# Batch 0 of an attention kernel with two feed-forward layers: v in sixteen transfers, dilated heads by halves of the sequence, and two leading feature tiles on 288, then 224 columns

## The chip, the cores and the metric

The kernel runs on one core of a Trainium2 chip. The metric is the device time of one execution in microseconds (us), as the median of several runs; lower is better. A profile belongs to one execution and gives the start and length of every instruction and of every DMA packet on that core. Five engines work side by side and wait for each other through semaphores only: PE (TensorE, matmuls; its weight loads are listed as PEld), DVE (VectorE), ACT (ScalarE), POOL (GpSimd) and SP (SyncE, here only a queue that issues DMAs). Each engine takes its instructions strictly in the order of its own list.

## The reference

Attention over 4 batches, 8 heads, 576 positions and 64 elements a head, then two feed-forward layers on all 2,304 tokens (512 to 2,048 to 512 elements), all in float32:

```python
scores = q @ k.T / 8                      # per batch and head
mask_plain = (rel >= 0) & (rel < 32)      # heads 0 to 3
mask_dil   = (rel >= 0) & (rel < 128) & (rel % 4 == 0)   # heads 4 to 7
attn = softmax(where(mask, scores, -1e9));  x = attn @ v  # tokens x 512
h = x @ w_in;   x = (h * sigmoid(1.702 * h)) @ w_out      # layer 1
h = x @ w_in2;  out = (relu(h) ** 2) @ w_out2             # layer 2
```

A query of a plain head sees the 32 positions up to its own. A query of a dilated head sees every fourth position of the last 128; the host therefore stores q, k and v of these heads as four runs of 144 positions (positions 0, 4, 8, ..., then 1, 5, 9, ..., and so on), and inside a run the mask is again a band of 32.

## The kernel before, in words

**Layout.** The host lays q and k out transposed and v by windows, for two halves u of 288 positions of each pair of heads (`qkv_in`). The tokens of the feed-forward layers are ordered by the same four runs: the first block of columns (`BLOCKS1[0]`, 512 tokens) holds runs 0, 1 and 2 of batch 0 whole (144 each) and 80 tokens of run 3. So columns 0 to 287 are runs 0 and 1, which for the dilated heads are the first half u = 0 of their stored sequence, and for the plain heads every fourth position from all of the sequence.

**Attention.** `attend` does one sub-step: four row groups of 32 queries (two halves or places of the sequence for two pairs of heads) by `nw` windows of 32 queries. Its chain is `scores` (PE, line 580), `maxima` (DVE, line 598, with the mask of `mask_band`), `exps` (ACT, line 605), the normalisation (lines 643 to 653), `turn` (a DVE transpose, line 667), `values` (PE, line 690, which needs v), and the copies of the result into the x tile as a rounded high part (line 316 or 318) and a remainder (line 707). Batch 0 has four sub-steps, `SUBS0`: windows 0 to 3 and 4 to 8 of both halves of the plain heads, then windows 0 to 4 and 5 to 8 of both halves of the dilated heads. Each pass of `values` waits for the one before it in this order and for the copies that empty its PSUM banks.

**Feed-forward.** `step` is one feature tile f (128 of 2,048 features): 12 `hidden` matmuls (lines 744 to 746; two weight parts and two x parts, four row blocks k of x), `tanh`, `times_h` (line 776), the split into high and remainder (lines 316 and 327), and 12 `project` matmuls (lines 801 to 803), each on up to 512 columns. Row blocks k = 0 and 1 of x are the plain heads, k = 2 and 3 the dilated ones. Weights come as raw tiles (`load_weights`, line 382), whose rounded parts are made by `top`, `join`, `high_part` and `low_part` on ACT and DVE.

**Loads of batch 0.** q and k of the plain heads come in pieces (lines 861 to 864), those of the dilated heads in one transfer for each half (line 884), v in eight transfers of 192 KB (`load_v0`, line 869), six issued by SP and two by ACT. All values of the plain heads wait for four of the eight, all of the dilated heads for the other four; scores of the dilated heads wait for both transfers of line 884.

**The order of all engines** is made in Python while the kernel is built: `Schedule.run` keeps, for each engine, the tasks whose predecessors are done, and takes the one that by its own cost table can start first and, among those about equal, the one with the smallest `want`. Constants such as `T_START`, `OFF`, `LEAD`, `AHEAD` set these wants and so the order alone. It also models eight DMAs in flight (`lanes`), counted over both issuing queues. Where PE would by this plan be idle ahead of the first feature tile, `keep_warm` (line 927) puts matmuls on zeros into its list, one for each 0.18 us (0.36 us in the first 6 us). `HALVES` = 0 means that every feature tile of the first block runs on all 512 columns; `opening` lets tiles 0 and 1 share a pair of PSUM banks so that their k = 0 and 1 matmuls can run before the dilated heads are done.

Of the kernel before, what the change touches and what calls it, by code (L numbers as in the profile page):

```python
# [9 lines left out]
BF16 = mybir.dt.bfloat16  # L10
# [9 lines left out]
P = 128  # L20
# [6 lines left out]
WIN = 32  # L27
KW = 2 * WIN
QB = 96
NBLK = 3  # L30
# [7 lines left out]
UQ, UK, UV = HALF, HALF + PAD, NBLK * P  # L38

T_START = 22.8  # L40
T_ATT = 1.86
# [6 lines left out]
AHEAD = (46, 54, 56)  # L48
# [7 lines left out]
PREP = 11.41  # L56

HALVES = 0
FIRST = 384
RAW_FROM = 2.32  # L60
NEXT_FROM = 22.83
OFF = (0.0, -2.48, 0.0, 0.0, 0.0, 0.0, 4.45, 0.0, 0.0, 0.0, 0.0, -7.43, -2.53, -7.14, -15.14, 0.23, -19.26, 0.0, 6.66, -23.27, 1.18, -0.52, -0.81, -0.26)
SHIFTED = ()
EARLY = 4
V_ACT = (1, 3)
V_PACKET = 0.09
WARM = 256
QK_FROM = -39.99
QK_STEP = 4.17
V_FROM = -22.79  # L70
V_STEP = 7.15
LEAD = (14.75, 2, 2)
# [4 lines left out]
SPARE_POOL = (0, 0, 3.41)  # L77
SPARE_ACT = (0.36, 0.36, 0)
SPARE_TO = (51.64, 211.81)
# [12 lines left out]
    (0, ((0, 0), (1, 0)), 4), (0, ((0, 4), (1, 4)), 5), (1, ((0, 0), (1, 0)), 5), (1, ((0, 5), (1, 5)), 4),  # L92
# [18 lines left out]
X_FROM = 4.93  # L111
X_WANT = 6.41
# [146 lines left out]
def attention_mlp_mlp(  # L259
# [8 lines left out]
    nc = tc.nc  # L268
# [18 lines left out]
    mask_band = att.tile([P, 5, KW], BF16, name="mask_band")  # L287
# [10 lines left out]
    v_first = [staged(f, 4 * NBLK * P).rearrange("k (t d) -> k t d", t=4 * NBLK) for f in (6, 5)]  # L298
# [60 lines left out]
    split_task = {}  # L359
# [42 lines left out]
    def weights(f, part, want, off):  # L402


        m = {}
# [33 lines left out]
        t = task("dma", 1.45, want - LEAD[0] + off[0], load, (), [raw_b], since=RAW_FROM)  # L439
# [18 lines left out]
    def x_pieces(b, pp, u, w0, nw):  # L458
# [3 lines left out]
        q0, q1 = (HALF * u + WIN * w0) // per, (HALF * u + WIN * (w0 + nw)) // per  # L462
        jobs = []
        for n, blk in enumerate(BLOCKS1):
            width = sum(e - a for _, _, a, e in blk)
            runs, col = [], 0
            for bb, r, a, e in blk:
                if bb == b:
                    lo, hi = (a, e) if plain else (r * ROW + a, r * ROW + e)
                    c = col - lo  # L470
                    lo, hi = max(lo, q0), min(hi, q1)
                    if lo < hi:
                        runs.append((r, lo - q0, hi - q0, c + lo))
                col += e - a
# [31 lines left out]
    def mask_of(pp, spec, i):  # L506
        w = spec[0][1] + i
        n = int(w == 0) if pp == 0 else {0: 2, 4: 3, 5: 4}.get(w, 0)
        return mask_band[:, n], n
# [4 lines left out]
    def attend(b, pp, spec, nw, want, n0, loads=None):  # L514
# [51 lines left out]
        def v_of(a, i):  # L566
            if first:
                t = spec[0][1] + i
                v, at = v_first[pp], 4 * NBLK - 1 if t == 3 * NBLK else t % 3 * NBLK + t // 3
            else:  # L570
                v, at = m["v"], i % 3 * 2 + i // 3
            return v[WIN * a:WIN * (a + 1), at]
# [98 lines left out]
        pieces = [(h, piece) for h in (1, 0) for piece in x_pieces(b, pp, *spec[h], nw)]  # L671
# [47 lines left out]
    def step(blk, f, want, a=0, z=None):  # L719
# [74 lines left out]
        for d in range(KD):  # L794

            def project(d=d):
# [10 lines left out]
                split_task[f, 1] + [hi, lo] + blk.setdefault(("last", a, d), []), [gh_b, gl_b, w_b, blk["o_buf"][d]],  # L807
# [34 lines left out]
    def spread_masks(part):  # L842
        n = slice(0, 2) if part == 0 else slice(3, 5)
        for a in (1, 2, 3):
            G.tensor_copy(mask_band[WIN * a:WIN * (a + 1), n], mask_band[0:WIN, n])
        if part == 0:
            G.tensor_copy(mask_band[:, 2], mask_band[:, 1])
            G.tensor_copy(mask_band[P // 2:P, 1], mask_band[P // 2:P, 0])
# [5 lines left out]
    band_tasks.append(band_tasks[0] + [task("pool", 1.1, -1999, lambda: spread_masks(1), mask_loads + band_tasks[0])])  # L854
# [34 lines left out]
    v0 = [[], []]  # L889
    for pp in range(2):  # L890
        for u, k in [(u, k) for u in range(2) for k in range(2)]:
            if pp == 0 and 2 * u + k in V_ACT:
                v0[pp].append(
                    task(
                        "act", 0.45, -900 + 2 * u + k, lambda u=u, k=k: load_v0(0, u, k, A), mask_loads + halves[0][1:], first_bs,
                        move=128 * V_PACKET / 16,
                    )
                )
            else:
                v0[pp].append(  # L900
                    early(
                        128 * V_PACKET / 16, V_FROM + V_STEP * pp + OFF[(8, 10)[u] + pp],
                        lambda u=u, k=k, pp=pp: load_v0(pp, u, k, nc.sync),
                    )
                )
# [648 lines left out]
```

## Time and profile before

| | |
|---|---|
| median of 3 runs | 811.39 us (810.5 to 811.91) |
| the profiled execution | 811.18 us, of which 809.4 us are the span from its first to its last instruction |
| mean granted TensorE clock | 0.994 of full speed |
| busy over the span | PE 98%, PEld 89%, DVE 66%, ACT 50%, POOL 1% |
| first feature matmul (line 744) | starts at 31.94 us |
| DMA | 172.63 MB, 213 GB/s over the span |

The page gives busy time by engine. The timeline lists instructions of one engine in order of time, like ones merged (x says how many), with the idle time before them and what ended it in brackets; "issue" there means that the profile shows nothing that the engine waited for. A queue named SPq or ACTq holds the instructions that issue DMAs. The windows view gives the busy time of each engine in a stretch, and what the DMAs moved.

### The profile page before, as it was taken

How to read it: one execution, taken by the hardware profiler on the slowest of the kernel's cores; microseconds unless marked ns; L12 is line 12 of the kernel's file. 1: busy time of each engine (PE TensorE's matmuls, PEld its weight loads, DVE VectorE, ACT ScalarE, POOL GpSimd, SP SyncE). 2: the span in 40 equal slices, each digit the busy share in tenths (PEclk: the TensorE clock that was granted, in tenths of full speed). 3: DMA queues.
4: the chain of work that ended last, by engine and by line, in shares of the span. 5: the costliest groups of instructions: out<-in, count | busy, mean ns of one | idle time of the engine just before them, and what ended most of it. 6: DMA issues, size and time to landing. Idle time of an engine off the chain costs nothing.

```text
span 809.4 us, 16460 instructions
## 1 busy us (share of the span) xinstructions
PE 796.7 (98%) x6570; PEld 722.4 (89%) x6570; DVE 534.5 (66%) x1170; ACT 406.6 (50%) x931; POOL 5.8 (1%) x17
## 2 busy tenths in 40 slices
PE   6899999999999999999999999999999999999998
PEld 5688888888899988888888999999999999999998
DVE  4788875443355588878887655689455699364774
ACT  5677765344444554444444255446355455354432
POOL 2000000000000000000000000000000000000000
PEclk9799999999999999999999999999999999999999
DMA  9577754221233369989576933695967686677741
GB/s 267 174 236 217 235 164 154 60 54 40 53 112 76 107 221 295 323 289 333 195 271 242 342 119 126 260 354 210 337 242 292 260 314 246 236 270 283 277 187 58
DMA packets 67963, 172.63 MB, mean 213 GB/s; under 512 B 5680, under 2 KB 43568, under 8 KB 62512
## 3 DMA queue, kind: packets, MB, share of 16 engines
q1 hardware_dynamic: 66880, 170.86, 61.3%
q8 instruction: 51, 0.84, 0.4%
q10 hardware_dynamic: 1008, 0.74, 0.3%
q14 instruction: 24, 0.20, 0.1%
HBM read 132.78 MB, written 38.80 MB: 212 GB/s over the span
## 4 chain that ended last, share of the span: by engine, by line
PE 97%; DMA 2%; issue 1%; DVE 0%; ACTq 0%
PE ps L744 8%; PE ps L801 8%; PE ps L745 8%; PE ps L802 8%; PE ps L803 8%; PE ps L746 8%; PE ps L1397 7%; PE ps L1242 7%; PE ps L1398 7%; PE ps L1241 7%; PE ps L1243 7%; PE ps L1396 7%; PE ps L690 2%; DMA first<-in_qkv 2%; PE ps L580 1%
## 5 line engine op out<-in xcount | busy, mean ns | idle before, releaser
L744 PE MATMUL ps<-x,wp 128*128 128x512 f32 (+1 forms) x320 | 119.3, 373 | 0.0
L801 PE MATMUL ps<-gh,wp 128*128 128x512 f32 (+1 forms) x320 | 119.1, 372 | 0.0
L745 PE MATMUL ps<-x,wp 128*128 128x512 f32 (+1 forms) x320 | 117.8, 368 | 0.0
L802 PE MATMUL ps<-gh,wp 128*128 128x512 f32 (+1 forms) x320 | 117.8, 368 | 0.0
L803 PE MATMUL ps<-gl,wp 128*128 128x512 f32 (+1 forms) x320 | 117.7, 368 | 0.0
L746 PE MATMUL ps<-x,wp 128*128 128x512 f32 (+1 forms) x320 | 117.7, 368 | 0.0
L1398 PE MATMUL ps<-gl,ws 128*128 128x384 f32 x336 | 112.2, 334 | 0.0
L1396 PE MATMUL ps<-gh,ws 128*128 128x384 f32 x336 | 112.2, 334 | 0.0
L1397 PE MATMUL ps<-gh,ws 128*128 128x384 f32 x336 | 112.2, 334 | 0.0
L316 ACT CAST gh<-gq 128x768 fp32r<-128x768 f32 x84 | 68.7, 838 | 73.5 <-PE ps L1397 49.8
L327 DVE TENSOR_TENSOR gl<-gq,gh 128x768 fp32r<-128x768 f32 x84 | 80.4, 957 | 29.2 <-PE ps L1398 22.2
L1241 PE MATMUL ps<-xo,ws 128*128 128x384 f32 x252 | 84.2, 334 | 0.0
L1242 PE MATMUL ps<-xo,ws 128*128 128x384 f32 x252 | 84.2, 334 | 0.0
L1243 PE MATMUL ps<-xo,ws 128*128 128x384 f32 x252 | 84.2, 334 | 0.0
L776 DVE SCALAR_TENSOR_TENSOR g<-g,ps 128x512 f32<-128x512 f32 (+1 forms) x80 | 50.2, 628 | 48.5 <-ACT g L773 48.0
L773 ACT ACTIVATE g<-ps 128x512 f32<-128x512 f32 (+1 forms) x80 | 44.1, 552 | 72.9 <-PE ps L746 72.3
L744 PEld LDWEIGHTS ps<-x,wp 128*128 128x128 f32 x320 | 60.3, 188 | 11.0 <-DVE x L707 0.2
L801 PEld LDWEIGHTS ps<-gh,wp 128*128 128x128 f32 x320 | 60.3, 188 | 10.4
L746 PEld LDWEIGHTS ps<-x,wp 128*128 128x128 f32 x320 | 60.3, 188 | 10.2
L803 PEld LDWEIGHTS ps<-gl,wp 128*128 128x128 f32 x320 | 60.3, 188 | 10.2
L802 PEld LDWEIGHTS ps<-gh,wp 128*128 128x128 f32 x320 | 60.3, 188 | 9.7
L745 PEld LDWEIGHTS ps<-x,wp 128*128 128x128 f32 x320 | 60.3, 188 | 9.5
(89 smaller groups left out, 1336.7 us busy)
## 6 DMA issues: line engine op xcount, KB each, us to landing
ws<-wo_s SPq DMA_DIRECT2D x42, 1024.0 KB, 7.1
ws<-wi_s SPq DMA_DIRECT2D x36, 896.0 KB, 6.3
raw<-in_w SPq DMA_DIRECT2D x60, 511.8 KB, 4.5
wo_s<-wt SPq DMA_DIRECT2D x16, 896.0 KB, 6.6
wi_s<-wt SPq DMA_DIRECT2D x16, 896.0 KB, 5.6
v<-in_qkv SPq DMA_DIRECT2D x48, 96.0 KB, 3.1
qk<-in_qkv SPq DMA_DIRECT2D x24, 192.0 KB, 3.4
xs<-x2d SPq DMA_DIRECT2D x12, 384.0 KB, 4.8
```

What stands on the lines that cost most here:

```text
L744: T.matmul(out, w_hi[:, ks], x[:, 0, k, a:z], start=(k == 0), stop=False)
L745: T.matmul(out, w_hi[:, ks], x[:, 1, k, a:z], start=False, stop=False)
L746: T.matmul(out, w_lo[:, ks], x[:, 0, k, a:z], start=False, stop=(k == KD - 1))
L801: T.matmul(out, w_hi[:, ds_], m["gh"], start=(f == 0 and a == 0), stop=False)
L802: T.matmul(out, w_lo[:, ds_], m["gh"], start=False, stop=False)
L803: T.matmul(out, w_hi[:, ds_], m["gl"], start=False, stop=(f == KF - 1))
L1241: T.matmul(out, wt[:, 0, a, ks], hi, start=(first and k == 0), stop=False, skip_group_check=True)
L1242: T.matmul(out, wt[:, 0, a, ks], lo, start=False, stop=False, skip_group_check=True)
L1243: T.matmul(out, wt[:, 1, a, ks], hi, start=False, stop=(k == 1), skip_group_check=True)
L1396: T.matmul(out, w[:, 0, j, ds_], hi, start=(first and j == 0), stop=False, skip_group_check=True)
L1397: T.matmul(out, w[:, 1, j, ds_], hi, start=False, stop=False, skip_group_check=True)
L1398: T.matmul(out, w[:, 0, j, ds_], lo, start=False, stop=(j == NPR - 1), skip_group_check=True)
```

## The change

v of batch 0 comes in sixteen transfers of 96 KB, all issued by SP. Each covers one row group of 32 partitions and six blocks of a sub-step's windows; each of the four sub-steps waits for its own four transfers.

The dilated heads are no longer cut by windows in both halves, but by halves of the sequence: the third sub-step does windows 0 to 4 and 4 to 8 of half 0, the fourth those of half 1. Each has five windows, so window 4 is done twice; the copy of its second result is left out (`skip`). Each waits only for its own half of q and k. Two more masks are made for it on POOL (kinds 5 and 6), since the two row groups of a sub-step now stand at different windows.

Feature tiles 0 and 1 run on columns 0 to 287 first and on columns 288 to 511 afterwards (`HALVES`, `FIRST`), so that each of their matmuls becomes two. The constants of the order are other ones.

```diff
-T_START = 22.8
-T_ATT = 1.86
+T_START = 25.83
+T_ATT = 2.23
-AHEAD = (46, 54, 56)
+AHEAD = (47, 54, 55)
-HALVES = 0
-FIRST = 384
-RAW_FROM = 2.32
+HALVES = 2
+FIRST = 288
+RAW_FROM = 4.07
-OFF = (0.0, -2.48, 0.0, 0.0, 0.0, 0.0, 4.45, 0.0, 0.0, 0.0, 0.0, -7.43, -2.53, -7.14, -15.14, 0.23, -19.26, 0.0, 6.66, -23.27, 1.18, -0.52, -0.81, -0.26)
+OFF = (-0.38, -9.86, -1.63, 6.74, 4.34, 1.09, 2.87, 0.0, 11.72, -1.21, 0.0, -0.97, -6.49, -4.91, -28.34, -0.79, -17.32, -6.24, -6.07, -20.82, 8.4, -0.29, -0.81, -0.26)
-V_FROM = -22.79
-V_STEP = 7.15
-LEAD = (14.75, 2, 2)
+V_FROM = -20.78
+V_STEP = 5.49
+LEAD = (16.66, 3.12, 2.25)
...
 SUBS0 = (
-    (0, ((0, 0), (1, 0)), 4), (0, ((0, 4), (1, 4)), 5), (1, ((0, 0), (1, 0)), 5), (1, ((0, 5), (1, 5)), 4),
+    (0, ((0, 0), (1, 0)), 4), (0, ((0, 4), (1, 4)), 5), (1, ((0, 0), (0, 4)), 5), (1, ((1, 0), (1, 4)), 5),
 )
...
-v_first = [staged(f, 4 * NBLK * P).rearrange("k (t d) -> k t d", t=4 * NBLK) for f in (6, 5)]
+v_plain = [staged(6, 6 * P).rearrange("k (t d) -> k t d", t=6) for _ in range(2)]
+v_other = [staged(5, 6 * P).rearrange("k (t d) -> k t d", t=6) for _ in range(2)]
...
-def x_pieces(b, pp, u, w0, nw):
+def x_pieces(b, pp, u, w0, nw, skip=0):
+    begun = q0 + WIN * skip // per
-                lo, hi = max(lo, q0), min(hi, q1)
+                lo, hi = max(lo, begun), min(hi, q1)
...
+        if spec[0][0] == spec[1][0]:
+            n = {0: 2, 1: 5, 4: 6}.get(w, 0)
+            return mask_band[:, n], n
...
-                split_task[f, 1] + [hi, lo] + blk.setdefault(("last", a, d), []), [gh_b, gl_b, w_b, blk["o_buf"][d]],
+                split_task[f, 1] + [hi, lo] + blk.setdefault(("last", a, d), blk.get(("last", 0, d), [])), [gh_b, gl_b, w_b, blk["o_buf"][d]],
...
-def load_v0(pp, u, k, on):
-    a, at = WIN * (2 * u + k), UQ + UK
-    src = qkv_in[0, 2 * pp + k, u, :, at:].rearrange("(c q) d -> q c d", q=WIN)
-    on.dma_start(v_first[pp][a:a + WIN].rearrange("q (c i) d -> q c (i d)", c=4), src)
+def load_plain_v(z, u, k):
+    a, at = WIN * (2 * u + k), UQ + UK + P * z
+    src = qkv_in[0, k, u, WIN * z:WIN * (z + 3), at:at + 2 * P].rearrange("(c q) d -> q c d", q=WIN)
+    nc.sync.dma_start(v_plain[z][a:a + WIN].rearrange("q (c i) d -> q c (i d)", c=3), src)
+def load_other_v(u, h, k):
+    a, at = WIN * (2 * h + k), UQ + UK + P * h
+    src = qkv_in[0, 2 + k, u, WIN * h:WIN * (h + 3), at:at + 2 * P].rearrange("(c q) d -> q c d", q=WIN)
+    nc.sync.dma_start(v_other[u][a:a + WIN].rearrange("q (c i) d -> q c (i d)", c=3), src)
...
 loads0 = [
-    {"qk": halves[0], "v": v0[0]}, {"qk": halves[0] + halves[1], "v": v0[0]},
-    {"qk": others[0] + others[1], "v": v0[1]}, {"qk": others[0] + others[1], "v": v0[1]},
+    {"qk": halves[0], "v": plain_v[0]}, {"qk": halves[0] + halves[1], "v": plain_v[1]},
+    {"qk": others[0], "v": other_v[0]}, {"qk": others[1], "v": other_v[1]},
 ]
```

By the new wants SP issues, after the transfers of line 884, v of the second plain sub-step, of half 0 of the dilated heads, of the first plain sub-step, one raw weight tile, v of half 1, and then the other raw tiles (before: all eight of v, then the raw tiles).

## Rows read from the trace of the kernel before

**Rows 1.** The page, engines: busy us, share of the span, instructions.
```profile
PE 796.7 (98%) x6570; PEld 722.4 (89%) x6570; DVE 534.5 (66%) x1170; ACT 406.6 (50%) x931; POOL 5.8 (1%) x17
```

**Rows 2.** Windows: busy us (instructions) by engine, PE clock, DMA share, GB/s.
```profile
32.00:232.00 200.00, 200.00 (x2174) 163.50 (x2173) 121.72 (x358) 115.27 (x341) 0.00 (x0) 1.00 0.43 129
232.00:262.00 30.00, 30.00 (x590) 28.98 (x589) 16.71 (x81) 13.60 (x63) 0.00 (x0) 1.00 0.32 86
```

**Rows 3.** Timeline of PE, 17 to 32 us: start, us, line, operands, count, wait.
```profile
17.06 0.30 PE L690 MATMUL ps<-first 32*64 32x32 f32 x3 [0.33 <-DMA first<-in_qkv]
19.46 1.35 PE L690 MATMUL ps<-first 32*64 32x32 f32 x69 [2.10 <-issue]
20.74 2.31 PE L927 MATMUL ps<-zeros 128*128 128x256 bf16 x10
22.98 1.02 PE L690 MATMUL ps<-first 32*64 32x32 f32 x49
25.66 1.01 PE L690 MATMUL ps<-first 32*64 32x64 f32 x47 [1.66 <-issue]
26.60 2.92 PE L927 MATMUL ps<-zeros 128*128 128x256 bf16 x14
29.45 0.91 PE L690 MATMUL ps<-first 32*64 32x32 f32 x66
31.56 0.46 PE L690 MATMUL ps<-first 32*64 32x64 f32 x30 [1.19 <-issue]
31.94 0.50 PE L744 MATMUL ps<-x,wp 128*128 128x512 f32 x1
```

**Rows 4.** The page, DMA queues: packets, MB, share of 16 engines.
```profile
q8 instruction: 51, 0.84, 0.4%
```

**Rows 5.** DMA queues, half-microsecond stretches from 16.5, 23.0, 28.5 and 32.5 us.
```profile
q8 instruction: 1, 0.02, 17.9%
...
q8 instruction: 1, 0.02, 12.8%
...
q8 instruction: 1, 0.02, 16.8%
...
q8 instruction: 1, 0.02, 17.1%
```

**Rows 6.** Timeline of SP's queue, 4 to 13 us.
```profile
4.78 1.02 SPq L884 DMA_DIRECT2D first<-in_qkv  x2
...
9.43 0.31 SPq L869 DMA_DIRECT2D first<-in_qkv  x1
...
12.50 0.31 SPq L869 DMA_DIRECT2D first<-in_qkv  x1
```

**Rows 7.** Line 884's two DMAs, from issue to landing.
```profile
DMA to landing us min/median/max: 4.6/5.8/7.1
```

**Rows 8.** Windows, columns as in rows 2.
```profile
0.00:4.00 4.00, 2.95 (x13) 1.75 (x13) 0.17 (x1) 0.67 (x1) 2.03 (x9) 1.00 0.53 136
4.00:8.00 4.00, 2.90 (x72) 2.17 (x72) 1.22 (x16) 1.06 (x3) 1.36 (x6) 1.00 0.99 287
8.00:12.00 4.00, 3.55 (x100) 2.56 (x97) 2.12 (x25) 3.99 (x24) 0.00 (x0) 1.00 1.04 323
```

**Rows 9.** Timeline of PE, feature matmuls on 512 columns, then on 256.
```profile
45.95 0.39 PE L744 MATMUL ps<-x,wp 128*128 128x512 f32 x1
...
57.28 0.39 PE L803 MATMUL ps<-gl,wp 128*128 128x512 f32 x1
...
239.93 0.28 PE L744 MATMUL ps<-x,wp 128*128 128x256 f32 x1
...
240.53 0.28 PE L746 MATMUL ps<-x,wp 128*128 128x256 f32 x1
```

**Rows 10.** Groups by line and form: a weight load; busy us, mean ns.
```profile
L745 PEld LDWEIGHTS ps<-x,wp 128*128 128x128 f32 x320 | 60.3, 188 | 9.5
```

**Rows 11.** Timeline of DVE: remainder of the first feature tile's activations.
```profile
41.34 0.69 DVE L327 TENSOR_TENSOR gl<-g,gh 128x512 fp32r<-128x512 f32 x1
```

More of the change, by code (lines that the diff above doesn't have):

```diff
@@ L55 @@
 ISSUE = 0.5
-PREP = 11.41
-HALVES = 0
-FIRST = 384
-RAW_FROM = 2.32
+PREP = 12
+HALVES = 2
+FIRST = 288
+RAW_FROM = 4.07
 NEXT_FROM = 22.83
-OFF = (0.0, -2.48, 0.0, 0.0, 0.0, 0.0, 4.45, 0.0, 0.0, 0.0, 0.0, -7.43, -2.53, -7.14, -15.14, 0.23, -19.26, 0.0, 6.66, -23.27, 1.18, -0.52, -0.81, -0.26)
+OFF = (-0.38, -9.86, -1.63, 6.74, 4.34, 1.09, 2.87, 0.0, 11.72, -1.21, 0.0, -0.97, -6.49, -4.91, -28.34, -0.79, -17.32, -6.24, -6.07, -20.82, 8.4, -0.29, -0.81, -0.26)
 SHIFTED = ()
 EARLY = 4
-V_ACT = (1, 3)
-V_PACKET = 0.09
+V_MOVED = 0.36
 WARM = 256
-QK_FROM = -39.99
-QK_STEP = 4.17
-V_FROM = -22.79
-V_STEP = 7.15
-LEAD = (14.75, 2, 2)
+QK_FROM = -40
+QK_STEP = 3.94
+V_FROM = -20.78
+V_STEP = 5.49
+LEAD = (16.66, 3.12, 2.25)
 SPACE = 5
@@ L76 @@
 IDLE = (0.25, 0.18)
-SPARE_POOL = (0, 0, 3.41)
-SPARE_ACT = (0.36, 0.36, 0)
-SPARE_TO = (51.64, 211.81)
+SPARE_POOL = (0.59, 0, 3.41)
+SPARE_ACT = (0.39, 0, 0)
+SPARE_TO = (51.64, 216.62)
 BLOCKS1 = [
@@ L110 @@
 X_EARLY = 17.0
-X_FROM = 4.93
-X_WANT = 6.41
+X_FROM = 2.64
+X_WANT = 6.14
 class Schedule:
@@ L285, in attention_mlp_mlp @@
     wo_s = dram.tile([7, P, 2, NPR, 256], F32, name="wo_s")
-    mask_band = att.tile([P, 5, KW], BF16, name="mask_band")
+    mask_band = att.tile([P, 7, KW], BF16, name="mask_band")
     first = {f: wpool.tile([P, 4096], F32, tag=f"wp{f}", bufs=1, name="first") for f in (4, 5, 6, 7)}
@@ L437, in low_part @@
             minus(e, wl[f, part], value(), wh[f, part])
-        t = task("dma", 1.45, want - LEAD[0] + off[0], load, (), [raw_b], since=RAW_FROM)
+        t = task("dma", 1.38, want - LEAD[0] + off[0], load, (), [raw_b], since=RAW_FROM)
         t = task(*TOP, want - LEAD[1] + off[1], top, [t] + tops_zero, [raw_b, c_b], True)
@@ L566, in v_of @@
         def v_of(a, i):
[L567 to L571, printed above, removed]
+            v = (v_other[spec[0][0]] if pp else v_plain[spec[0][1] > 0]) if first else m["v"]
+            at = i % 3 * 2 + i // 3
             return v[WIN * a:WIN * (a + 1), at]
@@ L670, in attend @@
         moved_of[n0] = [moved]
-        pieces = [(h, piece) for h in (1, 0) for piece in x_pieces(b, pp, *spec[h], nw)]
+        again = [0, int(spec[0][0] == spec[1][0])]
+        pieces = [(h, piece) for h in (1, 0) for piece in x_pieces(b, pp, *spec[h], nw, again[h])]
         for _, (n_, *_) in pieces:
@@ L845, in spread_masks @@
             G.tensor_copy(mask_band[WIN * a:WIN * (a + 1), n], mask_band[0:WIN, n])
+        if part == 1:
+            for kind, low, high in ((5, 0, 4), (6, 3, 0)):
+                G.tensor_copy(mask_band[0:P // 2, kind], mask_band[0:P // 2, low])
+                G.tensor_copy(mask_band[P // 2:P, kind], mask_band[P // 2:P, high])
         if part == 0:
@@ L853, in attention_mlp_mlp @@
     band_tasks = [[task("pool", 1.5, -2000, lambda: spread_masks(0), mask_loads[0:1])]]
-    band_tasks.append(band_tasks[0] + [task("pool", 1.1, -1999, lambda: spread_masks(1), mask_loads + band_tasks[0])])
+    band_tasks.append(band_tasks[0] + [task("pool", 2.0, -1999, lambda: spread_masks(1), mask_loads + band_tasks[0])])
     def load_half(u, z, on):
@@ L888, in attention_mlp_mlp @@
     ]
[L889 to L905, printed above, removed]
+    other_v = [[], []]
+    plain_v = [
+        [
+            early(V_MOVED, V_FROM + V_STEP * z + OFF[8 + 2 * z], lambda z=z, u=u, k=k: load_plain_v(z, u, k))
+            for u in range(2) for k in range(2)
+        ] for z in range(2)
+    ]
+    for u in range(2):
+        for h in range(2):
+            for k in range(2):
+                other_v[u].append(early(V_MOVED, V_FROM + V_STEP * (u + 2) + OFF[9 + 2 * u], lambda u=u, h=h, k=k: load_other_v(u, h, k)))
     loads0 = [
-        {"qk": halves[0], "v": v0[0]}, {"qk": halves[0] + halves[1], "v": v0[0]},
-        {"qk": others[0] + others[1], "v": v0[1]}, {"qk": others[0] + others[1], "v": v0[1]},
+        {"qk": halves[0], "v": plain_v[0]}, {"qk": halves[0] + halves[1], "v": plain_v[1]},
+        {"qk": others[0], "v": other_v[0]}, {"qk": others[1], "v": other_v[1]},
     ]
```

## The prediction

> **What bounds the kernel now.** The first view is the busy time by engine over long stretches [rows 2]: from 32 to 232 us PE is busy 200.00 of 200.00 us. From its first feature matmul on, PE never waits, and DVE and ACT are far from full. What follows 31.94 us is therefore a fixed amount of PE work, and the end is the start of the feature matmuls plus that work. A change to batch 0 can act in two ways: move this start, or change the amount of work behind it.
>
> The second view is PE's timeline ahead of that start [rows 3]. The reader is to see three holes in the passes of `values` (line 690): 17.36 to 19.46, 24.00 to 25.66 and 30.36 to 31.56, of 2.10, 1.66 and 1.19 us, 4.95 us together. Only ahead of the first stands a wait for q, k or v, 0.33 us, that ends at 17.06; the holes themselves have no releaser. They lie inside a pass that has already begun, and between them PE runs 69 + 10 + 49 = 128 and 47 + 14 + 66 = 127 matmuls: always the same count. The third view explains the count. The DMA queue called instruction moves 0.84 MB in 51 packets [rows 4] for 6,570 matmuls [rows 1], 129 matmuls a packet, with their weight loads. Its packets run in the half microseconds from 16.5, 23.0 and 28.5 us [rows 5], each 2.5 to 3.1 us ahead of the end of a hole. So I read the holes as PE waiting for its own next block of instructions. When a hole ends and the following block can be asked for, the packet comes about 3.6 us later (19.46 to 23.0) and 3.1 us later (25.66 to 28.5, at least 2.8); with the queues drained, 31.56 to 32.5, it takes 1.0 to 1.4 us. Blocks thus came at 19.46, 25.66 and 31.56, some 6 us apart, while 128 of these small matmuls are done in about 4. The start of the feature matmuls is set by that chain; it is 0.4 us behind the last link.
>
> [...]
>
> **The change part by part.** The profiled execution is 811.18 us, of which 809.4 are the span; the median is 811.39, so the sum may stand 0.2 low against it.
>
> *Third `scores` waits for one transfer of line 884, not two.* The two land between 4.6 and 7.1 us after issue [rows 7], so by about 9.4 and 12.5 us. PE may begin this pass some 2 us sooner, but the block of instructions that it runs into is the one ahead of the 19.46 us block; going back by 6.5 us, that one arrives at about 12.9. I cost this at nothing: PE stops at the block instead of at the transfer. Were the block there, it would give up to 2 us, which lies in the range.
>
> *v in sixteen.* The bytes are the same. What changes is how much is queued at 12.9 us, when the block of 19.46 is asked for. SP's queue shows the turn [rows 6]: the fifth v issue of SP waits until 9.43 and the sixth until 12.50 us, just the landings of the two transfers of line 884, which stand eight DMAs ahead of them if ACT's two are counted. So at most eight are in flight. Before, those waiting are 192 KB each. After, seven transfers of 96 KB can be issued by 9.43 and the eighth near 12.5: with q and k of batch 0 (2.49 MB, 608 columns x 128 x 4 bytes x 8) that is 3.18 MB. The DMAs moved 136 x 4 + 287 x 4 + 323 x 4 = 2.98 MB by 12.0 us [rows 8], and reach 3.2 at about 12.7. The queues are then nearly drained when PE asks at 12.9, and the nearest row is the packet at 32.5: 1.2 us from asking instead of 3.6. That gives 2.4 us on this link. The lower bound is nothing, if the packet waits as before; more than 2.4 from this link is excluded, as 1.2 is the shortest wait shown. The following links keep their 6.2 and 5.9 us, since raw weights fill the queues then as before. I take 2.4. The v of the first pass comes third, but four DMAs of 96 KB behind eight are landing near 17 us as before (17.06); later than that it eats into the gain.
>
> *Instruction count.* Sub-step four grows from four to five windows: 16 more records in its scores, hidden ahead of a block, and 16 more of `values` behind the start: at 0.91 / 66 us each [rows 3], 0.2 us. The first feature matmul stays behind the same block unless the matmuls on zeros fall by 45 or more; I take no change.
>
> *Two tiles in two parts.* 48 matmuls of 512 columns become 48 of 288 and 48 of 224. Fifty steps from 45.95 to 57.28 us give 0.2266 us at 512 columns, five from 239.93 to 240.53 give 0.120 at 256 [rows 9]; on the line through both, 288 take 0.133 and 224 take 0.107 us. That is 48 x (0.133 + 0.107 - 0.2266) = 0.6 us. The form with 224 is nowhere in the trace. Where 256 columns are run, weight loads are busy 28.98 of 30 us [rows 2], so I expect narrower ones to stay at the 0.120 of 256: 48 x (0.133 + 0.120 - 0.2266) = 1.3 us. The upper bound is a weight load laid bare, 0.188 us [rows 10]: 48 x (0.133 + 0.188 - 0.2266) = 4.5 us. I take 1.3, the nearest row.
>
> [...]
>
> *More pieces on DVE and ACT.* Activations of the two tiles come in two parts, two more windows in maxima and exps, four more mask copies on POOL. They lie beside PE's feature matmuls and the holes; price nothing while PE has matmuls ahead. That cover is thinner than before, which is the third rival.
>
> Sum: 811.18 - 2.4 + 0.2 + 1.3 = 810.3 us.
>
> **The rivals.**
>
> *Data, not instructions.* If the holes are waits for v (or anything else that sixteen smaller, better ordered transfers remove), up to all 4.95 us go: 811.18 - 4.95 + 1.5 = 807.7. [...] For it: the first hole stands right behind a wait for q, k or v. Against: the constant 128, and holes in the middle of passes whose v had been used already.
>
> *No help at the start.* The packets wait as long as before: 811.18 + 1.5 = 812.7. For it: at 12.9 us four more v transfers are just being issued, and a block asked for a little later meets them.
>
> *PE runs dry behind the start* (the other side). Before, the four tiles that fit the PSUM banks gave 4 x 12 x 0.2266 = 10.9 us of `hidden` work until the first `project` needed its activations, whose remainder is done at 42.03 us [rows 11], 10.1 us behind the start: covered. After, tiles 0 and 1 in two parts fill the same four banks with 24 x (0.133 + 0.120) = 6.1 us, and with the fourth `values` (96 records at 0.0138, 1.3 us) PE has 7.4. If DVE and ACT, which also prepare weights there, take the same 10.1 us, PE stands for 2.7 us: 810.3 + 2.7 = 813.0 with the gain at the start, 815.4 without it, say 813.8. It decides as soon as the remainder of the first part comes more than 7.4 us behind the first feature matmul. Against it: this part has 288 columns, and its `hidden` ends sooner.
>
> *Narrow matmuls are dear.* 4.5 instead of 1.3 us: 813.5.
>
> **How the numbers follow.** Forecast 0.40 (808.9 to 811.9), data 0.20, no help 0.16, PE dry 0.20, narrow 0.04. A measurement of this kernel tells about 0.2%, 1.6 us, from no change: faster is below 809.8, slower above 813.0. Faster: the data rival and half of the forecast's part, 0.41. Slower: the narrow rival, three quarters of PE dry and a little of no help, 0.20. Same: 0.39. The likeliest is 810.3. The range runs from the data rival with a little less split cost, 807.2, to PE dry with hardly a gain, 814.5, leaving out a tenth on either side.
>
> **What would show it.** Right: the holes still stand 127 or 128 matmuls apart, the first ends near 17 us instead of 19.46, the later ones near 23 and 29, the first line-744 matmul starts at 29 to 30 us, and the 224-column matmuls step by 0.12 us. Wrong: holes that vanish (data rival); a start at 31 to 32 us (no help); a gap of PE between line 744 and the first line 801 (PE dry); steps of the narrow matmuls near 0.19 us. The end of the kernel should differ from the start of its feature matmuls by the fixed work plus 1.5 us; any other difference means that a part of the order far behind has changed.

## The result, and the profile after

The changed kernel takes 816.63 us (median of 5 runs, 815.88 to 819.29) against 811.39 us (810.5 to 814.31) of the kernel before on the same chip: 1.006 times as long, 95% interval 1.0043 to 1.0077. It is 0.6% slower, clear of the noise; the prediction was 810.3 us, with a range that ended at 814.5. The profiled execution is 816.63 us with a span of 814.5 us, 5.1 more than before.

The page's engines line, to be held against [rows 1]: 86 matmuls more (48 of the split, 16 each of `scores` and `values`, 6 zeros), and nine instructions more on POOL, of 3.9 us.

```profile
PE 799.2 (98%) x6656; PEld 726.7 (89%) x6656; DVE 540.6 (66%) x1200; ACT 396.3 (49%) x909; POOL 9.7 (1%) x26
```

PE's timeline from 8 to 35 us of the changed kernel, columns as in [rows 3] (line 581 is `scores`, 692 `values`, 932 the zeros, 746 the first `hidden` line):

```profile
9.92 0.73 PE L581 MATMUL ps<-first 64*32 64x64 f32 x51 [0.66 <-DVE st L599]
12.70 0.45 PE L581 MATMUL ps<-first 64*32 64x64 f32 x29 [2.05 <-issue]
...
16.53 0.70 PE L932 MATMUL ps<-zeros 128*128 128x256 bf16 x5 [0.23 <-issue]
17.16 1.07 PE L692 MATMUL ps<-first 32*64 32x32 f32 x80
...
21.72 1.21 PE L692 MATMUL ps<-first 32*64 32x64 f32 x61 [1.26 <-issue]
22.86 2.38 PE L932 MATMUL ps<-zeros 128*128 128x256 bf16 x11
25.18 0.81 PE L692 MATMUL ps<-first 32*64 32x32 f32 x55
27.88 0.74 PE L692 MATMUL ps<-first 32*64 32x64 f32 x41 [1.89 <-issue]
28.56 2.53 PE L932 MATMUL ps<-zeros 128*128 128x256 bf16 x11
31.01 1.30 PE L692 MATMUL ps<-first 32*64 32x32 f32 x75
34.28 0.42 PE L692 MATMUL ps<-first 32*64 32x64 f32 x21 [1.96 <-issue]
34.63 0.40 PE L746 MATMUL ps<-x,wp 128*128 128x288 f32 x1
```

The holes without a releaser are still there, and still one block apart: 61 + 11 + 55 = 127 matmuls from 21.72 to 27.88, 41 + 11 + 75 = 127 from there to 34.28. All links came sooner than before: the block that ended the hole at 19.46 us [rows 3] is there at 16.53, those of 25.66 and 31.56 at 21.72 and 27.88. The instruction queue shows the turn that the prediction asked for, in the half microseconds from 13.5 and 19.0 us (after 12.70 and 16.53): the packet comes within 1.3 us of the end of a hole at 12.70, and 2.5 us or more behind the next one. That PE asks for a block when a hole ends is my reading of these intervals; the profile shows packets and holes, and no request.

```profile
q8 instruction: 1, 0.02, 12.9%
...
q8 instruction: 1, 0.02, 11.6%
```

What is new is the last hole. Ahead of the first feature matmul now stands the whole fourth pass of `values` (75 + 21 records, with 11 zeros before it), and in its middle one border more. Before, that tile came 30 records behind the border of 31.56 us; now it comes 21 records behind the one after.

PE's timeline behind the start, at its turns (288 columns, then 224, then the first `project`):

```profile
35.29 0.44 PE L747 MATMUL ps<-x,wp 128*128 128x288 f32 x1
...
38.41 0.39 PE L748 MATMUL ps<-x,wp 128*128 128x288 f32 x1
38.64 0.30 PE L746 MATMUL ps<-x,wp 128*128 128x288 f32 x1
...
39.43 0.27 PE L746 MATMUL ps<-x,wp 128*128 128x224 f32 x1
...
41.66 0.27 PE L748 MATMUL ps<-x,wp 128*128 128x224 f32 x1
41.77 0.30 PE L803 MATMUL ps<-gh,wp 128*128 128x288 f32 x1
```

From 35.29 to 38.41 us a matmul of 288 columns takes a step of 0.24 us, from 38.64 to 39.43 one of 0.79 / 6 = 0.132 us. The windows name the cause. Their columns here are the stretch and its length, PE's busy time and count, the granted clock as a share of full speed, DMA share and GB/s:

```profile
28.00:32.00 4.00, 4.00 (x122) 0.57 1.09 326
32.00:36.00 4.00, 2.04 (x54) 0.90 0.32 68
36.00:40.00 4.00, 4.00 (x24) 0.67 0.00 0
40.00:44.00 4.00, 4.00 (x63) 1.00 0.53 139
```

In half microseconds the clock is 1.00 from 32.0 to 35.0 us, 0.71 from 35.0, 0.50 from 35.5 to 38.5, 0.88 from 38.5 and 1.00 from 39.0: it fell about 0.9 us behind the end of the 1.96 us hole and was back at about 38.6 us. Below, the low clock is 0.50 and the high clock 1.00. In the kernel before it stands at 1.00 over all of 32 to 40 us.

The waits of PE from 31 us to the end are two; the second stands at 109 us:

```profile
PE ps L692 <- issue: 2.0, 1, 2.0
PE ps L692 <- DVE g L778: 0.6, 1, 0.6
```

**Where 5.1 us went.** The first feature matmul starts 34.63 - 31.94 = 2.69 us later, but has all of the fourth values behind it, 1.0 us of which PE did after the start before: 1.7 us net. Its 24 matmuls on 288 columns take 39.43 - 34.63 = 4.80 us, at the step of the high clock 24 x 0.132 = 3.17: 1.6 us. The 224-column step is (41.66 - 39.43) / 20 = 0.1115 us, so the split of two tiles costs 48 x (0.132 + 0.1115 - 0.2266) = 0.8 us. The stall at 109 us is 0.6. Together 4.7 of 5.1; 0.4 us is spread too thin to place. These are two executions, each within 0.3 us of its kernel's median.

### The profile page after: what moved, and what is told of

Read it like the earlier page. It is cut to its first block, busy times and chain, and to the rows that moved or that the text cites. A ratio compares the mean times of both kernels' runs of the same rounds, so it can differ in the third digit from the quotient of the medians.

```text
span 814.5 us, 16657 instructions
## 1 busy us (share of the span) xinstructions
PE 799.2 (98%) x6656; PEld 726.7 (89%) x6656; DVE 540.6 (66%) x1200; ACT 396.3 (49%) x909; POOL 9.7 (1%) x26
## 4 chain that ended last, share of the span: by engine, by line
PE 89%; DMA 4%; DVE 3%; ACT 2%; issue 1%; SPq 0%; ACTq 0%; DVEq 0%
PE ps L746 7%; PE ps L1401 7%; PE ps L1248 7%; PE ps L1246 7%; PE ps L1403 7%; PE ps L1247 7%; PE ps L1402 7%; PE ps L803 7%; PE ps L747 7%; PE ps L748 7%; PE ps L805 7%; PE ps L804 7%; DMA raw<-in_w 4%; PE ps L692 2%; PE ps L581 1%
## 5 line engine op out<-in xcount | busy, mean ns | idle before, releaser
L746 PE MATMUL ps<-x,wp 128*128 128x512 f32 (+3 forms) x328 | 121.3, 370 | 0.0
L803 PE MATMUL ps<-gh,wp 128*128 128x512 f32 (+3 forms) x328 | 120.6, 368 | 0.0
L747 PE MATMUL ps<-x,wp 128*128 128x512 f32 (+3 forms) x328 | 120.0, 366 | 0.0
L748 PE MATMUL ps<-x,wp 128*128 128x512 f32 (+3 forms) x328 | 119.8, 365 | 0.0
L805 PE MATMUL ps<-gl,wp 128*128 128x512 f32 (+3 forms) x328 | 119.3, 364 | 0.0
L804 PE MATMUL ps<-gh,wp 128*128 128x512 f32 (+3 forms) x328 | 119.2, 363 | 0.0
L778 DVE SCALAR_TENSOR_TENSOR g<-g,ps 128x512 f32<-128x512 f32 (+3 forms) x82 | 50.5, 616 | 48.1 <-ACT g L775 47.6
L775 ACT ACTIVATE g<-ps 128x512 f32<-128x512 f32 (+3 forms) x82 | 44.3, 542 | 75.2 <-PE ps L748 74.4
L746 PEld LDWEIGHTS ps<-x,wp 128*128 128x128 f32 x328 | 62.5, 190 | 10.7 <-DVE x L709 0.2
L748 PEld LDWEIGHTS ps<-x,wp 128*128 128x128 f32 x328 | 62.5, 191 | 9.8
L803 PEld LDWEIGHTS ps<-gh,wp 128*128 128x128 f32 x328 | 61.8, 188 | 10.2
L747 PEld LDWEIGHTS ps<-x,wp 128*128 128x128 f32 x328 | 62.5, 191 | 9.3
L804 PEld LDWEIGHTS ps<-gh,wp 128*128 128x128 f32 x328 | 61.8, 189 | 9.6
```

The source lines that it names most:

```text
L746: T.matmul(out, w_hi[:, ks], x[:, 0, k, a:z], start=(k == 0), stop=False)
L747: T.matmul(out, w_hi[:, ks], x[:, 1, k, a:z], start=False, stop=False)
L748: T.matmul(out, w_lo[:, ks], x[:, 0, k, a:z], start=False, stop=(k == KD - 1))
L803: T.matmul(out, w_hi[:, ds_], m["gh"], start=(f == 0 and a == 0), stop=False)
L804: T.matmul(out, w_lo[:, ds_], m["gh"], start=False, stop=False)
L805: T.matmul(out, w_hi[:, ds_], m["gl"], start=False, stop=(f == KF - 1))
```

## The experiments

Theory T: the first feature tile stands behind one border of blocks more than before; the hole there, and the low clock behind it, are the loss. Rivals: the split into 288 and 224 columns costs it; the order of the fourth values as such costs it; the matmuls on zeros are needed for the clock. No run leaves out a part of the computation. Each is timed in five rounds beside the kernel before on the same chip, whose medians were 812.42, 812.68 and 812.08 us for the three groups. The changed kernel itself was not timed again beside them, so a difference from its 816.63 us runs across groups; the ratios to the kernel before (the changed kernel's is 1.006) are the safer measure. A profile is one execution, and executions of one kernel lie up to 7 us apart (810.54 to 817.67 in g1); why they do is not shown. So the medians decide on times, and a profile shows places in one execution only.

**e1_tile_first.** The changed kernel; the fourth values wait for the 24 first matmuls.

```diff
+        if blk["i"] == 0 and f < 2 and a == 0:
+            t["next"].append(att_tasks[3])
+            att_tasks[3]["before"] += 1
```

> The changed kernel with one more dependence: the fourth pass of values may only run behind the 24 matmuls of feature tiles 0 and 1 on columns 0 to 287. Theory (order and instruction blocks): the change is slower because its order puts the fourth values (96 records) ahead of the first feature tile, so that PE must have one block of instructions more (the one that came at 34.28 us) before it may start. Then the first feature matmul starts at 30 to 31 us, as soon as its weights are split (30.5), and the time falls by 3 us or more, to 813 to 814. Rival (weights late): weights, not instructions, hold the first tile; the start stays at 33 us or later and the time at 816 to 817. Rival (the split itself): the start moves but the time stays above 815.

814.63 us, 1.0032 (1.0017 to 1.0048) of before, 2.0 less than the changed kernel. PE's timeline:

```profile
28.68 0.69 PE L692 MATMUL ps<-first 32*64 32x64 f32 x41 [1.69 <-issue]
29.31 3.24 PE L935 MATMUL ps<-zeros 128*128 128x256 bf16 x18
32.20 0.59 PE L746 MATMUL ps<-x,wp 128*128 128x288 f32 x1
```

The hole ahead of the tile is gone and the start is 2.4 us sooner. It is still not at the 30 to 31 us expected, nor the time at 813 to 814: 18 matmuls on zeros, put there for a gap in the plan, fill 2.9 us ahead of it. They do not cost all of that. The tile's third matmul needs the remainder of its weights, which DVE has done at 31.24 us; it starts at 32.83, so without the zeros it could come 1.6 us sooner at most. The rival of late weights is right to that extent.

**e2_after_wide_zeros and e3_before_wide_zeros.** Half as many matmuls on zeros, each twice as wide, in the changed kernel and in the one before.

```diff
-WARM = 256
+WARM = 512
-IDLE = (0.25, 0.18)
+IDLE = (0.25, 0.36)
```

> The changed kernel, with the matmuls on zeros twice as wide and half as many (512 columns, one for each 0.36 us of planned idle time), so that PE is kept busy about as long with 42 instructions pairs fewer ahead of the first feature tile (710 instead of 752). Theory (blocks): the first feature matmul no longer lies behind the block that came at 34.28; the hole of 1.96 us ahead of it goes, the start comes at 31.5 to 32.7 us and the time at 813.5 to 815. Rival (the holes are no instruction blocks, but data or DMA): the holes stay where they stand in the work, the start at 34.6 and the time at 816.6.

> The same edit on the kernel before: 38 matmuls on zeros fewer, so that its first feature matmul is number 596 instead of 634 and lies ahead of the block boundary near 604. Theory (blocks): the hole of 1.19 us in the third values goes, the holes inside the second values move towards its end, the start comes at 29.5 to 30.8 us instead of 31.94, and the time falls by 1 to 2 us to 809.3 to 810.4. Rival (no blocks): 811.4, holes in the same passes. A loss of TensorE's clock, with fewer instructions to keep it up, would show as a lower granted clock from 30 us on and could eat the gain.

e2: 814.15 us, 1.0035 (1.0017 to 1.0054). Only 710 records stand ahead of the tile, so the border at 731 now falls among its own first matmuls, where PE passes it without a hole, and the tile runs at the high clock (1.00 from 36 to 40 us, steps of 0.13 us behind its first). But it starts at 35.31 us, not at the 31.5 to 32.7 expected: with fewer early records the holes that ended at 12.70, 21.72 and 27.88 us in the changed kernel end at 14.66, 24.05 and 31.13 us. So what this profile gains on the changed kernel's (1.8 us of span) is the low clock and the stall at 109 us, not the start. e3: 812.07 us, 1.0002 (0.9987 to 1.0016): no difference, where 809.3 to 810.4 was expected. Its profiled execution, the fastest of its 12 at 809.5 us, has the places as expected. The hole in the third values is gone, the last one has moved to the end of the second, and line 744 starts at 29.98 us:

```profile
25.58 0.47 PE L690 MATMUL ps<-first 32*64 32x32 f32 x16 [2.95 <-issue]
...
29.98 0.50 PE L744 MATMUL ps<-x,wp 128*128 128x512 f32 x1
```

That holes move with the count of records is the theory's point, but the median gives no gain; on the time, e3 is inconclusive.

**e4_next_loads_late.** The changed kernel with the loads of batch 1's q, k and v later, so that less is queued when the last blocks are asked for.

```diff
-NEXT_FROM = 22.83
+NEXT_FROM = 32.0
```

> The changed kernel, with the loads of batch 1's q, k and v planned behind the eighth raw weight tile (1.1 MB that were issued from 22.7 to 31.7 us go to about 39 us and later). Theory (a block's packet waits in full DMA queues): the queues drain near 28 us, so the block asked for at 27.88 comes after some 4 us instead of 6.4, the hole ahead of the first feature tile shrinks from 1.96 us to 0 to 0.5, and the time falls by 1.5 to 2 us to about 815, unless the scores of batch 1 then come late. Rival (the packet's delay does not depend on the load, or the hole is no block): hole and start stay, 816.6 or more.

814.23 us, 1.0028 (1.0016 to 1.004). PE's timeline:

```profile
28.21 0.96 PE L692 MATMUL ps<-first 32*64 32x64 f32 x41 [2.54 <-issue]
29.10 2.53 PE L932 MATMUL ps<-zeros 128*128 128x256 bf16 x11
31.56 1.24 PE L692 MATMUL ps<-first 32*64 32x32 f32 x96
32.73 0.40 PE L746 MATMUL ps<-x,wp 128*128 128x288 f32 x1
```

The order is that of the changed kernel, record for record, up to the tile. Only the DMAs are emptier (0.11 instead of 1.09 of their time from 28 to 32 us): the packet comes in the half microsecond from 29.0, 0.8 to 1.3 us after 28.21, where the changed kernel's came in that from 31.0, 3.1 us or more after 27.88, and the fourth values run through. No hole, no low clock (1.00 from 32 to 40 us, the next eight steps are 0.13 us), and this execution is 812.34 us. That is the theory's plainest evidence: same list, a fuller queue, one hole more. The median still lies 0.28% above the kernel before, where the changed kernel's lies 0.6% above: about half of the loss goes with the hole and what hangs on it. Of the rest, the profiles place 0.8 us (spans of 810.2 and 809.4 us), about the price of the split.

**f1_no_halves.** The changed kernel without the split.

```diff
-HALVES = 2
+HALVES = 0
```

> The changed kernel with feature tiles 0 and 1 again on all 512 columns; v and the sub-steps stay as changed. Theory (the start is late because the first feature tile stands behind the fourth values, and so behind one block of instructions more): PE's list still has 752 records ahead of the first feature matmul, the holes still stand 127 or 128 apart, that matmul still starts at 34 to 35 us, and only the split's 0.74 us and what it does to the clock come back: 814 to 816 us. Rival (the split into 288 and 224 columns itself costs the time): a start as before or the loss gone, 811 to 812.5 us.

813.99 us, 1.0024 (1.0009 to 1.0038): 2.6 less than the changed kernel where 0.8 was the split's price. The profiled execution, the fastest of 12 at 811.97, has the hole in the same place:

```profile
33.27 0.42 PE L692 MATMUL ps<-first 32*64 32x64 f32 x21 [1.09 <-issue]
```

It is 0.9 us shorter, the start is at 33.62 us (34 to 35 was expected), and no low clock follows (1.00 from 32 to 40 us). A loss clear of the noise remains without the split, so the split is not the whole cause. But more than half of the loss goes with it, and its steps account for 0.8 us only. Whether the split also lengthens the hole and brings the low clock onto the tile, or executions differ in that by themselves, is not settled.

**f2_before_values_first.** The kernel before, its first tile behind the fourth values.

```diff
+            if (blk["i"], f, a, k) == (0, 0, 0, 0):
+                before = before + [att_tasks[3]]
```

> The kernel before with one thing changed: its first feature matmul is placed behind the whole fourth pass of values, as in the changed kernel. 724 records then stand ahead of it. Theory (the place in PE's list, counted in blocks of 127 or 128 records, sets the start): no block border lies between the old and the new place, so the start moves only by the 90 or so small records put ahead, some 1.2 to 2 us, which PE no longer does behind it: the end moves by less than 1 us unless a hole comes ahead of the tile; 811 to 813 us. Rival (it is the waiting for the fourth values as such that costs): 814 us or more, with a wait of PE for a named engine or DMA ahead of the tile.

822.16 us, 1.0112 (1.0087 to 1.0138). The time is the rival's, but the wait that it named did not come, and neither did the theory's time: there is no hole directly ahead of the tile, but it starts at 36.78 us, since 10 zeros, put into the planned gap, and 80 values, all at the low clock, now lie ahead of it (32.54 to 36.78 us, granted 0.50 from 32 to 36), and five of its first matmuls run at the low clock too (0.63 from 36 to 40 us). Behind it PE waits 2.5 us for DVE (line 707) before 200 us and 3.6 us for ACT (line 316) behind 400 us, waits that the kernel before does not have; what brings them was not followed. The place behind the fourth values costs time even without a border, by the zeros put ahead of it at least; so the theory names only a part of what this place costs, and the rival of the order stands in part.

**f3_tile_first_next and f4_before_next.** Batch 1's loads behind the eighth raw tile: with e1's edit (35.5), and in the kernel before (34.5).

> The changed kernel with the two first feature tiles (columns 0 to 287) ahead of the fourth values, and the loads of batch 1's q, k and v behind the eighth raw weight tile. Theory: both edits act on the chain of instruction blocks, one by standing one block earlier, the other by emptying the queues when a block is asked for; the last block ahead of the tile comes about 1.5 us sooner than with the order alone (28.7 us), the first feature matmul starts at 30.5 to 31.5 us, 812 to 813.5 us. Rival (either alone already gives all): 814 to 814.6 us.

> The kernel before with the loads of batch 1's q, k and v behind the eighth raw weight tile, nothing else. Theory (how much is queued in the DMAs sets how long a block of instructions takes): the last hole ahead of the first feature matmul ends 1 to 1.5 us sooner than 31.56 us, and all of it moves the end: 809.5 to 810.8 us. Rival (blocks do not depend on what is queued, or the first feature matmul then waits for something else): 811 to 812.5 us.

838.37 us, 1.0312 (1.0291 to 1.0332), and 818.65 us, 1.0072 (1.0054 to 1.009): both expectations fell. In f4 no hole stands behind 26.00 us any more: the packet comes 1.0 to 1.5 us after that, with the DMAs used for 0.13 of the time from 26 to 28 us, where the kernel before's came 2.8 to 3.3 us after 25.66. But 14 zeros and 96 values fill the time, and line 744 starts at 31.69 us, 0.25 sooner and not 1 to 1.5. Far behind, PE has a wait that the kernel before does not have; what in the planner's order brings it was not followed. PE's timeline of f4 at the second layer's first matmul:

```profile
462.24 0.52 PE L1241 MATMUL ps<-xo,wt 128*128 128x384 f32 x1 [5.12 <-ACT ost L322]
```

f3 has such a wait (4.04 us) and ten more microseconds of waits for DVE from 40 to 200 us. Its first tile starts at 33.78 us, where 30.5 to 31.5 was expected: the last hole ends at 29.22, no sooner than in e1, and 18 zeros follow. The two times say nothing of what the start is worth.

**g1_after_no_late_zeros and g2_before_no_late_zeros.** No matmuls on zeros where the plan's time is over 10 us; all else keeps its order.

```diff
-                if e == "pe" and self.idle and start - free[e] > IDLE[0]:
+                if e == "pe" and self.idle and start < 10 and start - free[e] > IDLE[0]:
```

> The changed kernel without the matmuls on zeros behind its third scores (53 of them fewer); the order of all else is the same, fourth values still ahead of the first feature tile. 699 records then stand ahead of the first feature matmul and all 24 of its first columns lie inside the block that ends at 731. Theory (the place of the first feature tile among the blocks costs the time): no hole directly ahead of the tile, the last hole ends at 27 to 28.5 us as before this edit, and the feature matmuls start at 29.5 to 31.2 us, some of them at the low clock: 812 to 814 us. Rival (the zeros only pay for the clock, the tile waits for its inputs anyway): start at 34 us or later, or a whole stretch of feature matmuls at the low clock, 816 us or more.

> The same cut on the kernel before: 51 matmuls on zeros fewer, 583 records ahead of the first feature matmul, which is now on the near side of the border at 603 with six matmuls and the first values behind them. Theory (blocks): the first feature matmul starts 1 to 4 us sooner than 31.94 us, but the hole that ended at 31.56 us stands behind it and is only covered by six matmuls of 0.23 us; a gain of 1 to 1.5 us if the clock stays up, none if the first tiles run at the low clock: 810 to 812.5 us. Rival (zeros keep the clock up and are worth their place): 813.5 us or more.

g1: 812.37 us, 1.0001 (0.9982 to 1.0019): as long as the kernel before with its zeros, with the split and the order of the changed kernel kept. Its timeline, then g2's:

```profile
25.83 1.65 PE L692 MATMUL ps<-first 32*64 32x32 f32 x88 [1.43 <-DVE x L709]
30.58 1.76 PE L692 MATMUL ps<-first 32*64 32x32 f32 x96 [3.10 <-DVE wp L327]
32.27 0.61 PE L746 MATMUL ps<-x,wp 128*128 128x288 f32 x1
```

```profile
25.37 0.63 PE L690 MATMUL ps<-first 32*64 32x32 f32 x18 [2.87 <-issue]
27.02 1.66 PE L690 MATMUL ps<-first 32*64 32x32 f32 x88 [1.02 <-DVE x L707]
28.61 0.80 PE L744 MATMUL ps<-x,wp 128*128 128x512 f32 x1
29.21 0.63 PE L745 MATMUL ps<-x,wp 128*128 128x512 f32 x1
...
30.91 0.63 PE L746 MATMUL ps<-x,wp 128*128 128x512 f32 x1
31.47 1.34 PE L690 MATMUL ps<-first 32*64 32x32 f32 x80
32.74 0.50 PE L744 MATMUL ps<-x,wp 128*128 128x512 f32 x1
```

In g1 the border at 731 lies behind the 24 first matmuls and no hole stands directly ahead of the tile; the price is that 19 of those matmuls run at the low clock (0.50 from 32 to 36 us). Ahead of the fourth values PE waits 3.10 us, so the start is 32.27 us, not the 29.5 to 31.2 expected. The profile puts this wait down to DVE's remainder of the weights (line 327), but no DVE instruction ends within 0.3 us of 30.58, and the copies that these values need are done at 29.63. The wait stands behind record 603, where the other runs have the border of 604, and that block's packet came in the half microsecond from 28.0, 2.1 to 2.6 us ahead of its end. So it is most likely a block once more. g2 takes the zeros out of the kernel before and is the version that beats both: 809.49 us, 0.9959 (0.9942 to 0.9975), below the 810 to 812.5 expected, with the tile 3.3 us sooner, at 28.61 us; six of its matmuls at 0.43 us and 80 values at the low clock (0.50 from 28 to 32 us) take back 1.5. The rival that zeros pay for themselves falls in both. But the change is not free without them: zeros cost time in both kernels, and with none planned after 10 us in either, the changed order (g1) is 2.9 us slower than the one before (g2), timed side by side.

**g3_loads_and_subs_alone and g4_loads_and_subs_no_zeros.** The changed kernel without the split and with the first six matmuls ahead of the fourth values, as before; g4 also without zeros behind the first 13 (`start < 6` in g1's line).

```diff
-HALVES = 2
+HALVES = 0
...
+            if (blk["i"], a, k) == (0, 0, 1) and f < 2:
+                t["next"].append(att_tasks[3])
+                att_tasks[3]["before"] += 1
```

> The changed kernel with feature tiles 0 and 1 on all 512 columns, and their first six matmuls ahead of the fourth values, as in the kernel before. What is left of the change is v in sixteen transfers, the sub-steps by halves of the sequence and the other constants. 663 records stand ahead of the first feature matmul, one border (604) fewer than in the changed kernel. Theory (the whole loss is the one block more, the low clock behind its hole and the split): start at 31 to 32.5 us, and 811 to 812.5 us, no different from the kernel before. Rival (smaller transfers or the sub-steps by halves themselves cost time): 814 us or more.

> The kernel of the run above without the matmuls on zeros behind the first 13: 589 records ahead of the first feature matmul, and its first twelve matmuls before the border at 604. Theory: the second border (349) and the third (477) come in later work, the first feature matmul starts at 27 to 30.5 us as soon as its weights and x are there, at the low clock at first; 809 to 812 us. Rival (without zeros the low clock takes back all that the blocks give): 812.5 us or more.

820.09 us, 1.0093 (1.007 to 1.0116), and 819.18 us, 1.0076 (1.0058 to 1.0093). Both have the wait of f4, line 1249 for ACT's line 322, 4.17 and 5.09 us at 463 us, with the clock at 0.71 to 0.95 around it; so whether v in sixteen and the halves of the sequence are neutral by themselves stays open, and both expectations of the time fell. What can be read is the start. g3's is 33.80 us, later than expected: the hole ends at 29.86 and 18 zeros follow. g4's timeline has no hole at the tile and shows what comes last instead:

```profile
28.58 0.79 PE L746 MATMUL ps<-x,wp 128*128 128x512 f32 x1 [1.04 <-ACT wp L316]
29.18 0.63 PE L747 MATMUL ps<-x,wp 128*128 128x512 f32 x1
30.31 0.79 PE L748 MATMUL ps<-x,wp 128*128 128x512 f32 x1 [0.51 <-DVE wp L327]
```

**One sum over the runs.** In f1's profile nothing is split, slowed or waited for behind the start, and the fourth values are done: span minus start is 809.9 - 33.62 = 776.3 us. For the others this should be 776.3 plus the split (0.8), what the first matmuls lose to the low clock, PE's waits behind the start, and values done behind it.

| profile | start | span - start | 776.3 + split + clock + waits + values | left |
|---|---|---|---|---|
| before | 31.94 | 777.5 | 0 + 0 + 0 + 1.0 = 777.3 | 0.2 |
| changed | 34.63 | 779.9 | 0.8 + 1.6 + 0.6 + 0 = 779.3 | 0.6 |
| e1 | 32.20 | 781.1 | 0.8 + 0.7 + 1.1 + 1.2 = 780.1 | 1.0 |
| e2 | 35.31 | 777.4 | 0.8 + 0.1 + 0 + 0 = 777.2 | 0.2 |
| e3 | 29.98 | 777.7 | 0 + 0 + 0 + 1.0 = 777.3 | 0.4 |
| e4 | 32.73 | 777.5 | 0.8 + 0.1 + 0 + 0 = 777.2 | 0.3 |
| g1 | 32.27 | 780.3 | 0.8 + 2.3 + 0.8 + 0 = 780.2 | 0.1 |
| g2 | 28.61 | 779.1 | 0 + 1.2 + 0 + 1.3 = 778.8 | 0.3 |

The start and four small terms carry each of these eight profiles to within 1 us; f2, f3, f4, g3 and g4, with their long waits far behind the start, are not among them. (The clock's term is the time of the 24, in g2 six, first matmuls less their steps at the high clock.)

## Why the prediction was wrong

**What bounds the kernel: right.** Behind the start PE is busy but for 0.6 us, and the end is the start plus the work. The reading of the holes as blocks of instructions holds: borders at the records 222, 349, 477, 604 and 731 of PE's list in the changed kernel, wherever PE is then, and e4 moves one by what is queued in the DMAs alone. The rival that the holes wait for data falls. Ahead of the first feature tile the holes are up to 2.05 us long in the changed kernel and 4.11 in e2. Behind the start, where 128 matmuls of 512 columns take 29 us (128 x 0.2266), no hole is left: PE's only wait there is the 0.6 us for DVE.

**The link at 12.9 us: right.** The block was asked for at 12.70, its packet came between 13.5 and 14.0, and the hole ended at 16.53 where some 17 was predicted. The windows of the changed kernel show the queues running low just there, if only for a moment (use of the DMAs 1.13, 0.56, 1.06):

```profile
12.50:13.00 0.50, 0.30 (x29) 1.00 1.13 234
13.00:13.50 0.50, 0.50 (x24) 1.00 0.56 117
13.50:14.00 0.50, 0.50 (x39) 1.00 1.06 246
```

The hole that ended at 19.46 us thus ends 2.9 us sooner, where more than 2.4 had been excluded, and the links behind it gained 3.9 and 3.7 us. So the rival that the packets wait as long as before falls too, though no gain reached the start.

**The failed step** is the one under the instruction count: "The first feature matmul stays behind the same block unless the matmuls on zeros fall by 45 or more; I take no change." I counted 16 + 16 records and zeros, and did not ask whether the order ahead of the tile stays. It did not: by the changed constants the whole fourth pass of values, 96 records and 11 zeros, goes ahead of the first feature tile, which stands at record 604 + 127 + 21 = 752 instead of 634, behind one hole more, of 1.96 us. e4 takes that hole away by an emptier queue, e1 by the order, g1 by fewer records, and each brings the start to 32.2 to 32.7 us. In time e4 and e1 take back about half of the loss (0.28 and 0.32% of 0.6 are left).

**The gain at the start was lost a second time.** I let 2.4 us of an earlier block pass straight to the start. Without the last hole the changed kernel would start at 34.63 - 1.96 = 32.67 us, 0.3 us better than before once the 1.0 us of values ahead is counted, though the third block came 3.7 us sooner. In its place came 11 zeros at the low clock (0.50 from 28.56 to 31.01 us), which the new order puts ahead of the fourth values. The weights stood close behind. DVE's timeline, remainder of the first weights, after and then before:

```profile
29.07 0.82 DVE L709 TENSOR_TENSOR x<-ps,x 128x256 fp32r<-128x256 f32 x2 [0.91 <-ACT x L316]
29.80 1.46 DVE L327 TENSOR_TENSOR wp<-first,wp 128x512 fp32r<-128x512 f32 x2
```

```profile
28.73 0.69 DVE L327 TENSOR_TENSOR wp<-first,wp 128x512 fp32r<-128x512 f32 x1 [0.49 <-ACT wp L316]
```

After, the first of the two, for tile 0, is done at 30.48 us (29.80 + 0.68) instead of 29.42. Its rounded part was there sooner than before: ACT has it at 27.94 us, where DVE before waited for ACT until 28.73. What comes ahead of it in DVE's list is the copies of the third values, and these wait for the hole that ends at 27.88. So this wait too hangs on a block, in part at least. g4 shows the weights as the wait that ends last once hole and zeros are out of the way.

**The clock was not in the sum.** No part of the prediction gave the first feature tiles the low clock; it cost another 1.6 us behind the hole right ahead of them, and in e4, with the same list and without that hole, it did not come.

**The split: right in kind, too dear.** 0.8 instead of 1.3 us: the 224-column step is 0.1115 us, nearer to the 0.107 of the line through both rows than to the 0.120 taken. The rival of dear narrow matmuls, with steps near 0.19, falls. The records of the weight loads there start 0.11 us apart too and are 0.19 us long, so they overlap; what sets this step is not shown.

**PE dry: did not happen.** The remainder of the first activations starts at 40.40 us, 5.8 us behind the start, and line 803 follows the last `hidden` matmul without a gap at 41.77. The low clock had lengthened that cover to 7.1 us, but e4, at the high clock, has no gap either with 5.6 us (32.73 to 38.33). That this rival forecast a loss, as came, is luck. Its cover was counted too large besides: 39 `hidden` matmuls stand ahead of the first line 801 (43.19 us) in the kernel before, and 45 ahead of the first 803 in the changed one, where it took 48 for each.

## What to carry to other kernels

Where a profile shows holes at a fixed count of instructions (here 127 or 128 matmuls), count the records of the new order up to the critical instruction, and not only the added ones; one pass moved ahead of it can put it behind one block more (here from record 634 to 752, behind a hole of 1.96 us). Then ask what else stands ahead of that instruction (weights, fillers put there for a planned gap) before passing a block's gain on. Matmuls on zeros are instructions too: here dropping those planned after 10 us made the kernel before 0.41% faster, though the mean granted clock of the profiled execution was 0.987 against 0.994. Where a trace names an engine for a wait, look whether that engine ended anything then: the count of records and the instruction packet can name a block instead (the 3.10 us of g1).

## What the runs showed of the hardware

From the end of a hole to the next instruction packet it took times that differ by a factor of about four: e4's packet came 0.8 to 1.3 us after 28.21 us, with the DMAs nearly idle (used for 0.11 of the time from 28 to 32 us), and the changed kernel's 3.8 to 4.3 us after 21.72 and 3.1 to 3.6 us after 27.88, with them in use for all of the time (1.02 from 21.72 to 25.5 us, 1.07 from 27.88 to 31). PE went on 1.9 to 3.3 us behind the packet in the changed kernel. The granted clock did not fall inside the hole of 1.96 us ahead of the first feature tile but about 0.9 us behind its end, whereas in the kernel before it fell inside the hole of 2.10 us that ends at 19.46 (0.89 from 18.5 to 19.0 us, 0.50 from there); with the same list and a hole of 1.09 us (f1) it stayed at 1.00 there.
